# One core, a retention layer and two mixture layers in one launch: lam is loaded from ScalarE's queue, and VectorE instead of GpSimd decays the first chunk's keys of five heads

## The chip, the cores and the metric

The kernel runs on one core of one Trainium2 chip. The time is the device time of one launch in microseconds (us); the number that counts is the median of several runs. A core has TensorE (PE; its weight loads are shown apart as PEld), VectorE (DVE), ScalarE (ACT), GpSimd (POOL) and SyncE (SP), and 16 DMA engines that all its queues share. SyncE here does nothing but start DMAs; ScalarE can start DMAs too, on a queue of its own.

## The reference

Three layers follow one another. Only the first matters for the change: a retention layer with one decay factor `lam` per head, worked through block by block with a running state `kv_state`.

```
for b in range(nb):
    intra = einsum('bhic,bhjc->bhij', qb, kb) * Dmask      # Dmask: powers of lam below the diagonal
    intra = einsum('bhij,bhjd->bhid', intra, vb)
    inter = einsum('bhid,bhde->bhie', qb * lam_pow, kv_state)
    out[:, :, sl] = intra + inter
    kb_dec = kb * rev_pow                                  # keys decayed by powers of lam
    kv_state = lam_block * kv_state + einsum('bhsd,bhse->bhde', kb_dec, vb)
```

There are 2 sequences of 768 positions and 8 heads of width 64. Two layers of matrix products come after it: a normalised two-matrix layer with residual (512 to 2048 to 512), and a routed attention over 4 experts.

## The kernel before

The retention layer is done in 12 chunks of 128 positions (6 for each sequence, taken in turn, so that chunk 0 and chunk 1 are both of the first sequence). Each chunk has two loads of 512 KB: `qk` (queries and keys, transposed; `load_qk`, L149) and `kvn` (keys and values; `load_kv`, L159). All loads are started by SyncE, on its one queue, in program order, several ahead of their use; a buffer that is still read holds back the load into it and all that stand behind it on the queue.

Everything that involves the decay is made from `lq`, a copy of `lam` (32 bytes) in each of the 128 partitions, loaded by one small DMA (L317). From `lq` VectorE makes `dec` with 8 scans, one for each head (L341), and GpSimd makes `qpow` with two copies and 7 doublings (L343, L346).

The first 20 to 50 us of the program are written out by hand: the string FRONT is a list of tokens that are emitted in that order, and the program order is the order on each engine (manual schedule). The tokens that matter here, each with the chunk's number n:

- `q:n`, `k:n`: start the load of `qk` or `kvn` of chunk n. The very first `qk` load stands right behind that of `lam`.
- `R:n`, `S:n`: scores `sc` on TensorE (L366, L370). `A:n`: `a` = scores times `dec` on VectorE (L401).
- `Ka:n`, `Kg:n`: the decayed keys `kd`; three heads by ScalarE (L389), the other five by GpSimd in one instruction (L395). There are two `kd` buffers.
- `T:n`: the chunk's share of the state, `ps`, on TensorE from `kd` and `kvn` (L415). `D:n` makes the state `st` from it on VectorE (L442, L444), `O:n` decays it to `old` on GpSimd (L450).
- `U:n`, `I:n`: the output `po` on TensorE, from the old state (L425) and from `a` (L434). `C:n` copies it to `xT` on ScalarE (L458, L460).

TensorE starts the program with ten matmuls on zeros (`warma`, L135), which feed nothing. Chunk 3's buffers are part of a tile named `early`. `g_sb` is a small constant that ScalarE loads (L693) for the layer behind. The order on TensorE is: `warma`, scores of chunk 0, `ps` of 0, `po` of 0, `ps` of 1, `ps` of 2, scores of 1 and 2, `po` of 1 and 2, and so on. Behind the retention layer TensorE goes on with the matmuls of the second layer (`h`, `y`) and of the third.

Of the kernel before, what the change touches and what calls it, by code (L numbers as in the profile page):

```python
# [14 lines left out]
ALU = mybir.AluOpType  # L15
AX = mybir.AxisListType

P = 128
B, H, S, D = 2, 8, 768, 64
# [55 lines left out]


FRONT = """
    k:0 Ka:0 Kg:0 k:1 k:2 Kg:1 q:1 R:0 Ka:1 A:0 Ka:2 T:0 D:0 I:0 C:0 Kg:2 O:0 T:1 T:2 D:1 S:1 q:2 w q:3 q:4 A:1 k:3
    k:4 S:2 A:2 Q:1 Q:2 O:1 D:2 Q:4 U:1 I:1 z:0 Q:3 O:2 l:0 t:0 U:2 I:2 C:1 w R:3 R:4 A:3 C:2 A:4 G Kg:3 ma:0 W mc:0
    mm:0 mi:0:0 h:0 r:0 k:5 q:5 U:3 I:3 e:0 Ka:3 T:3 Kg:4 k:6 D:3 O:3 Ka:4 T:4 S:5 A:5 U:4 C:3 q:6 Kg:6 q:7 sq:0:0  # L80
    Q:5 I:4 w z:1 mi:0:1 R:6 D:4 U:5 I:5 xs:0:0 k:7 xs:0:1 C:4 k:8 k:9 Ka:6 q:8 q:9 T:6 A:6 Q:7 C:5 I:6 D:6 k:10 p:0
# [17 lines left out]
def model(ctx, tc, qkT, kv, lam, g_ln, w12, wat, out):  # L99
    nc = tc.nc  # L100
# [31 lines left out]
    def warm(n, name):  # L132
        ps = ps_mid(f"warm{name}")
        for _ in range(n):
            nc.tensor.matmul(ps, zeros[:, :P], zeros, start=True, stop=True)  # L135
# [3 lines left out]
    R = {}  # L139
# [3 lines left out]
    def load_qk(n):  # L143
        b, c = order[n]
        if n % 4 == 3:
            qk = early[:, 0].rearrange("p (a h i) -> p a h i", a=2, h=HP)
        else:
            qk = r2.tile([P, 2, HP, P], F32, tag="qk", name=f"qk{b}{c}", bufs=3)
        nc.sync.dma_start(qk, qkT[b, c])  # L149
        R.setdefault((b, c), {})["qk"] = qk  # L150

    def load_kv(n):
        b, c = order[n]
        if n % 4 == 3:
            kvn = early[:, 1].rearrange("p (a h d) -> p a h d", a=2, h=H)
        else:
            kvn = r2.tile([P, 2, H, D], F32, tag="kvn", name=f"kvn{b}{c}", bufs=3)
        if c < NC - 1:
            nc.sync.dma_start(kvn, kv[b, c])  # L159
        else:  # L160
            nc.sync.dma_start(kvn[:, 1], kv[b, c, :, 1])
        R.setdefault((b, c), {})["kvn"] = kvn
# [56 lines left out]
    n, free_at = PLAN_FROM, 0  # L219
# [19 lines left out]
    def load_next(k=1):  # L239
        for _ in range(k):  # L240
            if to_load:
                to_load.pop(0)()
# [57 lines left out]
    def prep():  # L300
# [9 lines left out]
    lq = rc.tile([P, H], F32, tag="lq", name="lq")  # L310
    dec = rc.tile([P, H, P], F32, tag="dec", name="dec")
# [2 lines left out]
    by_hand = ExitStack()  # L314
    by_hand.enter_context(tc.manual_schedule(engines={
        mybir.EngineType.SP, mybir.EngineType.DVE, mybir.EngineType.Activation, mybir.EngineType.Pool}))
    nc.sync.dma_start(lq, lam.rearrange("h o -> o h").to_broadcast([P, H]))  # L317
    load_qk(0)
    g_sb = const.tile([P, KT], F32, tag="g", name="g_sb")
    table = const.tile([P, 1], F32, tag="table", name="table")  # L320
# [40 lines left out]
    def ret_scores(n, whole=False):  # L361
        r = R[order[n]]
        sc = r["sc"] = ps_big(f"sc{n}")
        for hp, h2 in HEADS:
            if whole:
                nc.tensor.matmul(sc[:, h2, cols(hp)], r["qk"][half(h2), 1, hp, :], r["qk"][half(h2), 0, hp, :],  # L366
                                 start=True, stop=True, skip_group_check=True)
                continue
            for kh in range(2):
                nc.tensor.matmul(sc[half(kh), h2, cols(hp)], r["qk"][half(h2), 1, hp, half(kh)],  # L370
                                 r["qk"][half(h2), 0, hp, :], start=True, stop=True, skip_group_check=True)

    def ret_qd(n):
        b, c = order[n]
        if c > 0:
            r = R[b, c]
            r["qd"] = r2.tile([P, HP, P], F32, tag="qd", name=f"qd{n}")
            nc.gpsimd.tensor_tensor(r["qd"], r["qk"][:, 0], qpow, ALU.mult)

    def ret_kd(n):  # L380
        r = R[order[n]]
        r["kd"] = r2.tile([P, H, D], F32, tag="kd", name=f"kd{n}")

    def ret_kd_some(n):
        r = R[order[n]]
        if "kd" not in r:
            ret_kd(n)
        for h in range(3):
            nc.scalar.mul(r["kd"][:, h, :], r["kvn"][:, 0, h, :], dec[:, h, P - 1:P])  # L389

    def ret_kd_rest(n):
        r = R[order[n]]
        if "kd" not in r:
            ret_kd(n)
        nc.gpsimd.tensor_tensor(r["kd"][:, 3:, :], r["kvn"][:, 0, 3:, :],  # L395
                                dec[:, 3:, P - 1:P].to_broadcast([P, H - 3, D]), ALU.mult)

    def ret_decay(n):
        r = R[order[n]]
        a = r["a"] = r2.tile([P, 2, HP, P], F32, tag="a", name=f"a{n}")  # L400
        nc.vector.tensor_mul(a, r["sc"].rearrange("p h (k i) -> p h k i", k=HP),  # L401
                             dec.rearrange("p (h k) i -> p h k i", h=2))
# [5 lines left out]
    def ret_state(n):  # L408

        b, c = order[n]  # L410
        r = R[b, c]
        if c < NC - 1:
            ps = r["ps"] = ps_mid(f"ps{n}")
            for hp, h2 in HEADS:
                nc.tensor.matmul(ps[half(h2), cols(hp, D)], r["kd"][:, h2 * HP + hp, :],  # L415
                                 r["kvn"][:, 1, h2 * HP + hp, :], start=True, stop=True, skip_group_check=True)

    def ret_outer(n):
        b, c = order[n]
        r = R[b, c]  # L420
        r["po"] = ps_big(f"po{n}")
        if True:
            st = ST.pop(n - 1)
            for hp, h2 in HEADS:
                nc.tensor.matmul(out_at(r["po"], hp, h2), st[half(h2), hp, :], r["qd"][half(h2), hp, :],  # L425
                                 start=(hp < 2), stop=False, skip_group_check=True)

    def ret_inner(n):
        b, c = order[n]
        r = R[b, c]  # L430
        if c == 0:
            r["po"] = ps_big(f"po{n}")
        for hp, h2 in HEADS:
            nc.tensor.matmul(out_at(r["po"], hp, h2), r["kvn"][:, 1, h2 * HP + hp, :], r["a"][:, h2, hp, :],  # L434
                             start=(c == 0), stop=True, skip_group_check=True)

    def ret_sum(n):
        b, c = order[n]
        st = ST[n] = r2.tile([P, HP, D], F32, tag="st", name=f"st{n}")
        pv = R[b, c]["ps"][:, :HP * D].rearrange("p (h e) -> p h e", h=HP)  # L440
        if c == 0:
            nc.vector.tensor_copy(st, pv)  # L442
        else:
            nc.vector.tensor_tensor(st, pv, ST["old"], ALU.add)  # L444

    def ret_old(n):
        st = ST[n]
        if True:
            ST["old"] = r2.tile([P, HP, D], F32, tag="old", name=f"old{n}", bufs=1)
            nc.gpsimd.tensor_tensor(ST["old"], st, qpow[:, :, P - 1:P].to_broadcast([P, HP, D]), ALU.mult)  # L450
# [26 lines left out]
    def ln_copy(blk, name):  # L477
        s4 = LN[name, blk] = lnp.tile([P, TB], F32, tag="s4", name=f"{name}s{blk}")
        nc.scalar.copy(s4, LP.pop((name, blk))[:, :TB])
# [193 lines left out]
    def do(op, *a):  # L673
        if op == "q":
            load_qk(*a)
        elif op == "k":
            load_kv(*a)
        elif op == "w":
            load_next()
        elif op == "S":  # L680
            ret_scores(*a)
        elif op == "R":
            ret_scores(*a, whole=True)
        elif op == "A":
            ret_decay(*a)
        elif op == "Ka":
            ret_kd_some(*a)
        elif op == "Kg":
            ret_kd_rest(*a)
        elif op == "Q":  # L690
            ret_qd(*a)
        elif op == "G":
            nc.scalar.dma_start(g_sb, g_ln)  # L693
        elif op == "W":
            warm(WARM[1], "b")
        elif op == "U":
            ret_outer(*a)
        elif op == "T":
            ret_state(*a)
        elif op == "I":  # L700
            ret_inner(*a)
        elif op == "D":
            ret_sum(*a)
        elif op == "O":
            ret_old(*a)
        elif op == "C":
            ret_copy(*a)
        elif op == "ma":
            ln_sums(*a, "mu")
        elif op == "mc":  # L710
            ln_copy(*a, "mu")
        elif op == "mm":
            ln_mean(*a)
        elif op == "mi":
            ln_minus(*a)
        elif op == "xs":
            ln_high(*a)
        elif op == "lo":
            ln_low(*a)
        elif op == "sq":  # L720
            ln_square(*a)
        elif op == "va":
            ln_sums(*a, "va")
        elif op == "vc":
            ln_copy(*a, "va")
        elif op == "vd":
            ln_out(*a)
        elif op == "P":
            begin(a)
        elif op == "LA":  # L730
            LEAVE[a][0]()
        elif op == "LD":
            LEAVE[a][1]()
        elif op == "X":
            rp.close()
            rest_of_room()
        elif op == "park":
            park(*a)
        else:
            PARTS[a[0]]["zlthrep".index(op)]()  # L740
# [329 lines left out]
```

## Time and profile before

| | |
|---|---|
| median of 3 runs | 448.39 us (448.27 to 448.59) |
| profiled execution | 448.26 us; its span, from the first to the last instruction, 446.5 us |
| TensorE (PE) busy | 440.2 us, 99% of the span |
| VectorE, ScalarE, GpSimd busy | 314.2 us, 201.7 us, 38.0 us |
| DMA, 0 to 60 us | 16.94 MB, 282 GB/s |

The profile is of one execution. Busy time is the time in which an engine's instructions were running; a bracket at the end of a row tells how long the engine had been idle before it and what ended the idle time. Times are counted from the start of the span.

### The profile page before, as it was taken

What the parts mean: (1) busy time and instruction counts of PE and PEld (TensorE: products, weight loads), DVE (VectorE), ACT (ScalarE), POOL (GpSimd) and SP (SyncE); (2) the same over time, 40 slices, a digit from 0 to 9 for tenths busy, and PEclk for the clock granted to TensorE, in tenths of its full rate; (3) what the DMA queues carried; (4) which work ended last, traced back from release to release, by engine and by line L of the source; (5) the groups of instructions that cost most, each with busy time, mean ns of one, the idle gap of its engine ahead of it and who ended that gap; (6) DMA issues with size and microseconds to landing.
All of it is one profiled execution on the core that took longest, in us unless ns stands there. A gap on an engine that the chain in (4) does not pass through costs nothing.

```text
span 446.5 us, 9085 instructions
## 1 busy us (share of the span) xinstructions
PE 440.2 (99%) x3714; PEld 414.0 (93%) x3715; DVE 314.2 (70%) x622; ACT 201.7 (45%) x464; POOL 38.0 (9%) x64
## 2 busy tenths in 40 slices
PE   8999999999999999999999999999999999999997
PEld 5678889999999999999999999999999998999885
DVE  4689899859768778626799936556657485756753
ACT  4488765445433213202324612212146657747872
POOL 7655200000000000000000000000000100001000
PEclk9999999999999999999999999999999999999999
DMA  7985643514321231201132531211000000001012
GB/s 294 391 332 214 189 144 112 182 41 155 130 94 54 88 95 51 91 0 46 50 102 87 186 99 52 73 56 35 1 1 0 1 2 2 25 25 48 25 72 97
DMA packets 15226, 41.81 MB, mean 94 GB/s; under 512 B 2240, under 2 KB 5072, under 8 KB 15184
## 3 DMA queue, kind: packets, MB, share of 16 engines
q1 hardware_dynamic: 14896, 41.10, 27.1%
q8 instruction: 29, 0.48, 0.4%
q10 hardware_dynamic: 288, 0.13, 0.1%
q14 instruction: 13, 0.11, 0.1%
HBM read 34.90 MB, written 6.32 MB: 92 GB/s over the span
## 4 chain that ended last, share of the span: by engine, by line
PE 94%; DMA 2%; ACT 1%; POOL 1%; DVE 1%; issue 0%; DVEq 0%; ACTq 0%
PE h L556 30%; PE y L592 28%; PE pj L818 8%; PE av L961 4%; PE pv L833 4%; PE o L988 4%; PE s L896 4%; PE t L949 3%; PE po L434 2%; PE yf L614 2%; PE sc L366 1%; DMA kvn<-in_kv 1%; PE po L425 1%; PE mean L483 1%; DMA lq<-in_lam 1%; PE ps L415 1%
## 5 line engine op out<-in xcount | busy, mean ns | idle before, releaser
L556 PE MATMUL h<-xn,w 128*128 128x384 f32 x768 | 138.5, 335 | 0.0
L556 PEld LDWEIGHTS h<-xn,w 128*128 128x128 f32 x768 | 133.5, 188 | 1.4 <-issue 0.6
L592 PE MATMUL y<-hs,w 128*128 128x384 f32 x552 | 99.7, 334 | 0.0
L592 PEld LDWEIGHTS y<-hs,w 128*128 128x128 f32 x552 | 96.1, 188 | 0.0
L575 ACT ACTIVATE hs<-h 128x384 fp32r<-128x384 f32 x50 | 24.5, 491 | 113.6 <-PE h L556 104.1
L578 DVE SCALAR_TENSOR_TENSOR hs<-h,hs 128x384 fp32r<-128x384 f32 x50 | 27.7, 554 | 33.2 <-ACT hs L575 33.2
L600 DVE TENSOR_TENSOR xT<-xT,y 128x768 f32<-128x768 f32 x24 | 22.8, 951 | 27.3 <-PE y L592 27.3
L920 POOL TENSOR_TENSOR wide<-c,gw 128x256 f32<-128x256 f32 x12 | 7.3, 612 | 382.2 <-DVE c L917 359.0
L818 PE MATMUL pj<-x,wa 128*128 128x384 f32 x192 | 35.1, 338 | 0.0
L818 PEld LDWEIGHTS pj<-x,wa 128*128 128x128 f32 x192 | 33.3, 188 | 0.5 <-ACT gw L859 0.2
L278 ACT CAST w<-top 128x512 fp32r<-128x512 f32 x32 | 19.8, 618 | 30.4 <-DVE top L270 30.4
L951 ACT COPY aT<-t 128x384 f32<-128x384 f32 (+5 forms) x68 | 28.1, 467 | 8.2 <-PE t L949 8.1
L261 ACT ACTIVATE mag<-raw 128x512 f32<-128x512 f32 x31 | 20.5, 669 | 7.9 <-DVE w L289 4.1
L286 DVE TENSOR_TENSOR top<-top,w 128x512 f32<-128x512 f32 x32 | 21.9, 684 | 0.8 <-ACT w L278 0.8
L289 DVE TENSOR_TENSOR w<-top,mag 128x512 fp32r<-128x512 f32 x32 | 22.0, 686 | 0.3
L283 DVE SCALAR_TENSOR_TENSOR mag<-raw,mag 128x512 f32<-128x512 uint32 x31 | 21.4, 689 | 0.7
L270 DVE SCALAR_TENSOR_TENSOR top<-raw,mag 128x512 int32<-128x512 int32 x31 | 21.4, 689 | 0.6
L961 PE MATMUL av<-aT,v 128*64 128x128 f32 x336 | 20.6, 276 | 0.0
L903 ACT ACTIVATE att<-s,negm 128x384 f32<-128x384 f32 (+3 forms) x32 | 16.7, 531 | 7.8 <-DVE negm L901 7.4
L896 PE MATMUL s<-k,qs 64*128 64x384 f32 (+4 forms) x192 | 20.1, 334 | 0.0
L961 PEld LDWEIGHTS av<-aT,v 128*64 128x64 f32 x336 | 18.1, 137 | 1.5 <-issue 1.0
L949 PEld LDWEIGHTS t<-ident,att 64*128 64x128 f32 x336 | 14.8, 138 | 4.7 <-issue 2.8
(140 smaller groups left out, 622.5 us busy)
## 6 DMA issues: line engine op xcount, KB each, us to landing
raw<-in_w SPq DMA_DIRECT2D x31, 512.0 KB, 3.7
qk<-in_qkT SPq DMA_DIRECT2D x9, 512.0 KB, 7.6
kvn<-in_kv SPq DMA_DIRECT2D x8, 512.0 KB, 6.6
xd<-xT SPq DMA_DIRECT2D x4, 768.0 KB, 8.0
xr<-xd SPq DMA_DIRECT2D x8, 384.0 KB, 3.1
out<-os SPq DMA_DIRECT2D x11, 256.0 KB, 2.0
early<-in_qkT SPq DMA_DIRECT2D x3, 512.0 KB, 7.9
rawa<-in_wat SPq DMA_DIRECT2D x3, 512.0 KB, 3.3
```

Source lines behind the costliest of these rows:

```text
L286: nc.vector.tensor_tensor(t["top"], t["top"], t["w"][:, 0].bitcast(F32), ALU.subtract)
L289: nc.vector.tensor_tensor(t["w"][:, 1], t["top"], t["mag"], ALU.add)
L556: nc.tensor.matmul(ph[:, :TB], w[:, wi, k, :], xn[:, xi, k, :], start=(i == 0), stop=(i == 11))
L575: LAST.append([nc.scalar.activation(h[:, 0], ph[:, :TB], AF.Relu)])
L578: LAST[-1].append(nc.vector.scalar_tensor_tensor(h[:, 1], ph[:, :TB], 0.0, h[:, 0].bitcast(F32), ALU.max, ALU.subtract))
L592: nc.tensor.matmul(y[:, j, :TB], w[:, wi, e * P:(e + 1) * P], h[:, xi], start=(f == 0 and i == 0), stop=(f == GF - 1 and i == 2))
L600: nc.vector.tensor_tensor(xv, xv, y[:, :, :TB], ALU.add)
L818: nc.tensor.matmul(ps[:, :TB], w[:, wi, k, :], x2[:, xi, k, :], start=(i == 0), stop=(i == 11))
L896: nc.tensor.matmul(banks[h][c], q[r, qi], k[r, ki, pr, c * m:(c + 1) * m], start=(i == 0), stop=(i == 2))
L949: nc.tensor.transpose(pt[r][:, j], x[half(r)], ident[half(r), half(r)])
L951: nc.scalar.copy(aT[:, :, r], pt[r])
L961: nc.tensor.matmul(row["pav"][half(e2), pr * P:(pr + 1) * P], v[:, j, e * HD:(e + 1) * HD], row["aT"][pr][:, (e2 * (t + 1) + j) * P:(e2 * ...
```

## The change

The load of `lam` is started by ScalarE, on ScalarE's own DMA queue, and no longer by SyncE. `Kg:0`, the decay of the first chunk's keys of heads 3 to 7, becomes `Kv:0`: the same instruction on VectorE. The other chunks keep GpSimd.

```
 FRONT = """
-    k:0 Ka:0 Kg:0 k:1 k:2 Kg:1 q:1 R:0 Ka:1 A:0 Ka:2 T:0 D:0 I:0 C:0 Kg:2 O:0 T:1 T:2 D:1 S:1 q:2 w q:3 q:4 A:1 k:3
+    k:0 Ka:0 Kv:0 k:1 k:2 Kg:1 q:1 R:0 Ka:1 A:0 Ka:2 T:0 D:0 I:0 C:0 Kg:2 O:0 T:1 T:2 D:1 S:1 q:2 w q:3 q:4 A:1 k:3
...
-    nc.sync.dma_start(lq, lam.rearrange("h o -> o h").to_broadcast([P, H]))
+    nc.scalar.dma_start(lq, lam.rearrange("h o -> o h").to_broadcast([P, H]))
     load_qk(0)
...
-    def ret_kd_rest(n):
+    def ret_kd_rest(n, engine):
         r = R[order[n]]
         if "kd" not in r:
             ret_kd(n)
-        nc.gpsimd.tensor_tensor(r["kd"][:, 3:, :], r["kvn"][:, 0, 3:, :],
-                                dec[:, 3:, P - 1:P].to_broadcast([P, H - 3, D]), ALU.mult)
+        engine.tensor_tensor(r["kd"][:, 3:, :], r["kvn"][:, 0, 3:, :],
+                             dec[:, 3:, P - 1:P].to_broadcast([P, H - 3, D]), ALU.mult)
...
         elif op == "Kg":
-            ret_kd_rest(*a)
+            ret_kd_rest(*a, nc.gpsimd)
+        elif op == "Kv":
+            ret_kd_rest(*a, nc.vector)
```

On ScalarE, at the very start of the program (`table` is a one-column copy that brings in the activation table; the branch is the program's first jump, whose line number alone has changed):

```order
-L1066 UNCONDITIONAL_BRANCH
+L1068 UNCONDITIONAL_BRANCH
+L317 DMA lq<-in_lam 128x8
 L321 ACT_TABLE_LOAD
 L321 CAST table<-zeros 128x1
```

The start of the DMA comes ahead of everything that ScalarE does; it waits for nothing. On SyncE, at the same place, the first row goes and the loads of chunk 0 are the first that its queue gets:

```order
-L1066 UNCONDITIONAL_BRANCH
-L317 DMA lq<-in_lam 128x8
+L1068 UNCONDITIONAL_BRANCH
 L149 DMA qk_113<-in_qkT 128x1024
 L159 DMA kvn_162<-in_kv 128x1024
```

On VectorE, from the program's start to the first chunk's state (kd of chunk 0 is named `kd_164`, its `kvn` `kvn_162`):

```order
 L130 MEMSET zeros 128x256
 L341 SCALAR_TENSOR_TENSOR dec<-lq,hit 128x128 x8
+L395 TENSOR_TENSOR kd_164<-kvn_162,dec 128x320
 L401 TENSOR_TENSOR a_189<-sc_177,dec 128x1024
 L442 COPY st_204<-ps_195 128x256
```

The decay of five heads' keys now stands between the eight scans and `a` of chunk 0; on GpSimd the same row is gone from its place behind the last doubling of `qpow`.

## Rows read from the trace of the kernel before

**Rows 1.** Windows: busy us (instructions) of PE, PEld, DVE, ACT, POOL; clock; DMA share; GB/s.

```profile
40.00:60.00 20.00, 20.00 (x249) 17.62 (x248) 18.15 (x30) 15.32 (x34) 5.04 (x5) 1.00 0.50 166
60.00:300.00 240.00, 240.00 (x1392) 237.44 (x1391) 174.88 (x311) 80.66 (x145) 0.00 (x0) 1.00 0.28 88
```

**Rows 2.** The chain that ended last, its first 50 us: start, us, what.

```profile
0.74 2.72 DMA lq<-in_lam
...
9.31 0.74 POOL kd L395
...
10.09 0.68 PE ps L415 x14
...
11.87 1.24 DVE a L401
...
29.42 5.35 DMA kvn<-in_kv
```

**Rows 3.** Timeline, 0 to 14 us: start, us, engine, instruction, count [idle before].

```profile
0.74 0.39 SPq L317 DMA_DIRECT2D lq<-in_lam  x1
...
1.19 0.41 SPq L149 DMA_DIRECT2D qk<-in_qkT  x1
...
3.56 2.85 DVE L341 TENSOR_TENSOR_SCAN dec<-lq,hit 128x128 f32<-128x128 f32 x8 [2.43 <-DMA lq<-in_lam]
...
4.05 2.76 POOL L346 TENSOR_TENSOR qpow<-qpow 128x4 f32<-128x4 f32 x7
...
4.86 0.44 SPq L149 DMA_DIRECT2D early<-in_qkT  x1
...
5.56 1.02 PEld L366 LDWEIGHTS sc<-qk 64*128 64x128 f32 x16 [0.84 <-DMA qk<-in_qkT]
...
6.68 0.82 ACT L389 ACTIVATE kd<-kvn,dec 128x64 f32<-128x64 f32 x3 [4.46 <-DMA kvn<-in_kv]
6.78 0.72 POOL L395 TENSOR_TENSOR kd<-kvn,dec 128x320 f32<-128x320 f32 x1
...
6.83 1.22 DVE L401 TENSOR_TENSOR a<-sc,dec 128x1024 f32<-128x1024 f32 x1 [0.43 <-PE sc L366]
...
10.09 0.54 PEld L415 LDWEIGHTS ps<-kvn,kd 128*64 128x64 f32 x14 [0.24 <-POOL kd L395]
```

**Rows 4.** DMA packets of 2.2 to 3.3 us, then of 3.4 to 4.4 us.

```profile
DMA packets 103, 0.07 MB, mean 62 GB/s; under 512 B 87, under 2 KB 87, under 8 KB 103
...
DMA packets 93, 0.38 MB, mean 381 GB/s; under 512 B 0, under 2 KB 0, under 8 KB 93
```

**Rows 5.** ScalarE's other early DMA; then chunk 3's `qk`: KB, us to landing.

```profile
16.62 0.39 ACTq L693 DMA_DIRECT2D g_sb<-in_g_ln  x1
...
early<-in_qkT SPq DMA_DIRECT2D x1, 512.0 KB, 9.8
```

**Rows 6.** DMA by queue (q1 SyncE's, q10 ScalarE's), 19.9 to 21.9 us; then 21.9 to 23.1.

```profile
q1 hardware_dynamic: 211, 0.77, 96.9%
q10 hardware_dynamic: 138, 0.00, 4.1%
...
q10 hardware_dynamic: 6, 0.00, 0.5%
```

**Rows 7.** VectorE by line and form, 0 to 60 us: count, busy us, mean ns, idle before.

```profile
L444 DVE TENSOR_TENSOR st<-ps,old 128x256 f32<-128x256 f32 x8 | 3.4, 419 | 2.6 <-POOL old L450 2.0 <-PE ps L415 0.6
...
L286 DVE TENSOR_TENSOR top<-top,w 128x512 f32<-128x512 f32 x3 | 2.1, 684 | 0.0
```

**Rows 8.** Lines 500 and 450 alone: shortest/median/longest ns, first and last start.

```profile
L500 DVE SCALAR_TENSOR_TENSOR xn<-dq,g_sb,xn x8: 608/612/1083, 30.8 to 51.0; 128x384 fp32r<-128x384 f32 x8
...
L450 POOL TENSOR_TENSOR old<-st,qpow x8: 621/638/941, 10.0 to 43.9; 128x256 f32<-128x256 f32 x8
```

**Rows 9.** Timelines of VectorE and GpSimd at 30 us.

```profile
30.83 0.98 DVE L500 SCALAR_TENSOR_TENSOR xn<-dq,g_sb,xn 128x384 fp32r<-128x384 f32 x1
...
30.46 0.94 POOL L450 TENSOR_TENSOR old<-st,qpow 128x256 f32<-128x256 f32 x1
```

## The prediction

> **What bounds the kernel now.** The windows come first [rows 1]: from 40 us on TensorE is never idle, 20.00 of 20.00 us and then 240.00 of 240.00. What comes earlier or later at 40 us therefore comes earlier or later at the end, and the change sits in the first 10 us. Next the chain that ended last [rows 2]. It begins with the load of `lam`, goes through GpSimd, the first chunks' states on TensorE, VectorE's `a` of chunk 1 and, from 29.42 us, the load of chunk 9's keys, which starts when TensorE has freed the buffer. So the start is a chain of TensorE with short stalls, and it begins with `lam`. The timeline shows the first links [rows 3]: `lam` is issued at 0.74 us and has landed at 0.74 + 2.72 = 3.46 [rows 2]; VectorE's eight scans run from 3.56 to 6.41; GpSimd's doublings run from 4.05 to 6.81; the first `qk` lets TensorE's scores start at 5.56; the first keys are there at 6.68; `a` of chunk 0 starts at 6.83.
>
> **What the change takes away.** SyncE's queue loses one issue: the first `qk` is issued at 0.74 instead of 1.19, and all the loads behind it can be 0.45 us earlier [rows 3]. Little of that can be used. Earlier scores are of no use, since `a`, which takes them, also needs the scans; these depend on `lam` alone and end at 6.41 at the earliest. The place that can use it is chunk 2: its five decayed heads run on GpSimd from 9.31 [rows 2], and TensorE stands idle 0.24 us for them [rows 3]. With chunk 2's keys 0.45 us earlier, and one instruction of 0.72 us less on GpSimd [rows 3], that stall goes: **-0.24**. ScalarE issues `lam` ahead of its activation table; it is idle for 4.46 us before its first decayed keys [rows 3], so the 0.39 us of issuing costs nothing; without that idle time it would cost these 0.39.
>
> **What it adds on VectorE.** The decay of 320 columns goes in front of `a`. VectorE does 256 columns in 419 ns and 512 in 684 [rows 7], so 320 take 419 + 265/4 = 485 ns. Before, VectorE was idle for 0.43 us ahead of `a` [rows 3], so most of it is hidden, if nothing else is in the way. Something is. The decay reads two operands from SBUF while GpSimd's last doubling still runs, until 6.81. Where such a pair met [rows 9], both were longer: VectorE's line 500 took 0.98 us (median 612 ns), GpSimd's line 450 took 0.94 (median 638) [rows 8]. That is 0.3 to 0.37 us each. The doubling leaves 6.81 - 6.41 = 0.40 us to be met, so the wait lies between 0 and 0.40; I take 0.25, because a part of the doubling's time is its start. `a` then starts at 6.41 + 0.05 + 0.49 + 0.25 = 7.20 instead of 6.83, **+0.37**, and `po` of chunk 0 and all behind it on TensorE with it.
>
> On this wait the Trainium skill (SBUF — State Buffer, section "Who interferes with whom") is stricter: a VectorE instruction with two SBUF inputs and a GpSimd one that reads SBUF exclude each other for the whole instruction. By that the wait would be the full 0.40 and the sum 0.15 higher.
>
> **What it does to the arrival of `lam`.** This is the largest term, and the trace holds no case of two loads that start together on two queues. Before, `lam`'s 128 small rows stood alone at the head of the only queue; the loads of chunk 0 came behind them. Now they start at the same time as 512 KB of `qk` on the other queue, on the same 16 engines. Two things are to be seen. First, the first rows of `qk` are slow: from 2.2 to 3.3 us there are 103 - 87 = 16 large packets, one for each engine, at 62 GB/s; from 3.4 us on the rate is 381 [rows 4]. Full rate thus comes 2.2 us after the issue at 1.19, and would come at 2.95 after an issue at 0.74. Second, the one other load that ScalarE issues early is as small as `lam`: `g_sb`, issued at 16.62 in the middle of SyncE's traffic [rows 5]. Its packets pass from 19.9 us on between the large ones, 138 small to 211 large in 2.0 us, and the last six only after 21.9 [rows 6]. It took over 5.3 us instead of `lam`'s 2.72. A small transfer on the second queue is not let past the large ones.
>
> The price: an engine has 128/16 = 8 rows of `lam`. If each waits for one large packet, and a large packet takes 16 x 2.0/211 = 0.152 us [rows 6], the eight need 1.2 us from 2.95 on, which is 4.15; with 0.25 from the last row to the landing it is 4.4 instead of 3.46: **+0.95**. The bounds: below 0, if `lam`'s rows get through while the first rows of `qk` are still on their way; an earlier landing than 3.46 is excluded, since ScalarE can't issue before 0.74 and there is nothing that would make 128 rows faster than alone. Above, as `g_sb`: up to 23.1 - 16.62 = 6.5 us, which is 3.8 more. I take 0.95 because the queues are still empty at the start, while `g_sb` met a full one. The scans and the doublings both hang on `lam`, so both move by it, and `a` with them.
>
> **Other waits.** By the order of the changed program ScalarE's `g_sb` DMA now waits for chunk 3's `qk` load to land; that is 4.86 + 9.8 = 14.7 us [rows 3, 5], well before 16.62, so nothing behind it on ScalarE (its copy of the first means, the next decayed keys) is held. Chunk 4's key load now waits for VectorE instead of GpSimd to have read chunk 0's keys; it waits for `po` of chunk 0 anyway, which comes after both.
>
> **The sum.** +0.95 (`lam`) + 0.37 (VectorE) - 0.24 (stall of chunk 2) = +1.08 us at `ps` of chunk 2. From there the chain is TensorE, `a` of chunk 1 at 11.87, TensorE, and the load at 29.42 that TensorE itself releases [rows 2]; I see no wait on it for something that does not move along, so it is carried to 40 us and to the end. The profiled execution took 448.26: 449.34. It lies 0.13 below the median of the runs, 448.39, so I predict 449.5. A change within 0.2% (0.90 us, 447.49 to 449.29) is about what a measurement of this kernel can't tell from none.
>
> **The rivals.**
> - *`lam` is not delayed* (on the other side: not slower). Its eight rows on each engine pass before the first row of `qk` has its data. Then only -0.24 and VectorE's 0.12 to 0.52 remain: -0.12 to +0.28, so 448.3 to 448.7, no change that can be told. For it speaks that the engines move next to nothing until 3.3 us [rows 4]; against it, that those first 16 packets occupy them all the same. It decides as long as `lam` lands less than 0.75 us late. The Trainium skill (DMA: Bandwidth & Descriptors, section "Queues, rings and completion order") speaks for this rival: an engine takes turns between its queues by whole packets of some 9 to 17 descriptors, so that all of `lam`'s rows on an engine could go in one turn. The trace of `g_sb` rather shows single rows between large ones.
> - *`lam` comes behind a backlog*, as `g_sb` did: SyncE keeps issuing 512 KB every 0.45 us, and `lam` waits behind two or more of them. 2 to 3.8 us late gives 450.5 to 452.3.
> - *The earlier loads pay off.* Every wait for a load goes down by 0.45, `lam` comes in time and VectorE's decay meets nothing: 447.9. To be faster by more than 0.2% it would need twice what the queue gives; TensorE's waits in this stretch are single ones of 0.2 to 0.3 us like the 0.24 of chunk 2 [rows 3].
>
> **How the numbers follow.** The forecast case (`lam` 0.7 to 1.4 us late) gives 0.7 - 0.12 to 1.4 + 0.28 = +0.6 to +1.7, so 449.0 to 450.1; chance 0.50, of which 0.08 lie within 0.2%. `lam` not delayed: 0.30, all within. The backlog: 0.10, slower. The pay-off: 0.10, of which 0.04 beyond 0.2%. Slower 0.42 + 0.10 = 0.52; same 0.08 + 0.30 + 0.06 = 0.44; faster 0.04. The range from 448.2 to 450.4 takes in the first two cases and leaves out the rest of the other two; the forecast's own range is 449.0 to 450.1.
>
> **What would show it.** `lam` landed, and the first scan started, near 4.4 us instead of 3.46: this step alone decides. VectorE's decay of 0.5 us, or 0.7 where it meets the last doubling; `a` of chunk 0 near 8.2; no stall of TensorE for chunk 2's GpSimd keys; the chunk 9 load issued near 30.5; the first `h` matmuls some 1.1 us later than before. The prediction is wrong if `lam` lands before 4.2 us, or if a wait behind 10 us is for something that has not moved and takes up the delay.

## The result, and the profile after

The changed kernel takes 452.58 us (median of 5 runs, 451.72 to 453.02) against 448.39: a ratio of 1.0092 with a 95% interval of 1.0081 to 1.0103. It is slower by 0.9%, which is the sign that was forecast, but 452.58 lies 3.1 us above the predicted 449.5 and outside the range of 448.2 to 450.4. The profiled run took 451.72 us, its span 449.9 us, 3.4 more than before.

The chain that ended last, in the changed kernel (start, us, what), answers to [rows 2]:

```profile
0.74 5.45 DMA lq<-in_lam
...
9.17 0.72 DVE kd L395
9.90 1.14 DVE a L401
...
11.08 1.97 PE po L434 x16
...
16.75 0.67 PE po L425 x16
...
32.87 5.22 DMA kvn<-in_kv
```

It begins with `lam` as before, but `lam` lands at 0.74 + 5.45 = 6.19 us, where it landed at 3.46: +2.73. The first matmuls of `U` for chunk 1 (L425) go from 13.24 to 16.75, +3.51, and the load of chunk 9's keys from 29.42 to 32.87, +3.45. The sixteen matmuls of chunk 0's `po` (L434) take 1.97 us; before they took 1.09. The first `h` matmuls of the second layer go from 39.62 to 43.06, +3.44. These are the rows of the timeline of before for `po`, `U` and `h`, and last that of the changed kernel for `h`:

```profile
8.11 1.09 PE L434 MATMUL po<-a,kvn 128*64 128x128 f32 x16
...
13.24 0.67 PE L425 MATMUL po<-qd,st 64*64 64x128 f32 x16 [0.30 <-DVE a L401]
...
39.62 1.66 PE L556 MATMUL h<-xn,w 128*128 128x384 f32 x8
...
43.06 1.14 PE L556 MATMUL h<-xn,w 128*128 128x384 f32 x5
```

The first 12 us of the timeline (start, us, engine, instruction, count, idle before) answer to [rows 3]:

```profile
0.74 0.41 ACTq L317 DMA_DIRECT2D lq<-in_lam  x1
0.74 0.39 SPq L149 DMA_DIRECT2D qk<-in_qkT  x1
...
6.06 1.48 PE L366 MATMUL sc<-qk 64*128 64x128 f32 x16 [0.43 <-DMA qk<-in_qkT]
...
6.29 2.85 DVE L341 TENSOR_TENSOR_SCAN dec<-lq,hit 128x128 f32<-128x128 f32 x8 [5.16 <-DMA lq<-in_lam]
6.79 2.76 POOL L346 TENSOR_TENSOR qpow<-qpow 128x4 f32<-128x4 f32 x7
...
9.17 0.72 DVE L395 TENSOR_TENSOR kd<-kvn,dec 128x320 f32<-128x320 f32 x1
9.51 0.98 POOL L395 TENSOR_TENSOR kd<-kvn,dec 128x320 f32<-128x320 f32 x1
9.82 1.21 DVE L401 TENSOR_TENSOR a<-sc,dec 128x1024 f32<-128x1024 f32 x1
...
9.95 0.96 PE L415 MATMUL ps<-kvn,kd 128*64 128x64 f32 x14 [1.66 <-DVE kd L395]
```

Three things are to be seen. The first `qk` is issued 0.45 us earlier, and yet the scores that need it start 0.50 us later, 6.06 instead of 5.56: the large load came late too, not only the small one. `a` of chunk 0 starts at 9.82 instead of 6.83, +2.99, so VectorE's extra decay adds only 2.99 - 2.73 = 0.26. And TensorE is idle for 1.66 us ahead of `ps`. The DMA packets of 2.2 to 3.3 us, and then of 3.4 to 4.4 us, answer to [rows 4] (q1 is SyncE's queue, q10 ScalarE's; packets, MB, share of the 16 engines):

```profile
DMA packets 80, 0.18 MB, mean 161 GB/s; under 512 B 37, under 2 KB 37, under 8 KB 80
...
q1 hardware_dynamic: 43, 0.18, 58.1%
q10 hardware_dynamic: 37, 0.00, 1.7%
...
DMA packets 70, 0.13 MB, mean 128 GB/s; under 512 B 39, under 2 KB 39, under 8 KB 70
...
q1 hardware_dynamic: 35, 0.13, 50.5%
q10 hardware_dynamic: 35, 0.00, 1.6%
```

Where the kernel before moved 381 GB/s, this one moves 128, and the two queues pass packets in equal numbers: in 1.0 us 35 of `lam`'s rows on q10, and 35 on q1, of which 31 are large (39 packets are under 512 B, the 35 rows and 4 others). The windows (busy us and instructions of PE, PEld, DVE, ACT, POOL; granted clock; DMA share; GB/s) answer to [rows 1]:

```profile
9.00:10.00 1.00, 0.05 (x2) 0.05 (x2) 0.96 (x3) 0.61 (x3) 1.00 (x2) 1.00 1.05 430
10.00:11.00 1.00, 0.91 (x14) 0.72 (x14) 1.00 (x2) 0.00 (x1) 0.48 (x1) 0.59 1.02 418
11.00:12.00 1.00, 0.92 (x10) 0.92 (x11) 0.37 (x2) 0.82 (x3) 0.95 (x2) 0.50 1.04 422
12.00:13.00 1.00, 1.00 (x14) 1.00 (x14) 0.00 (x0) 0.00 (x0) 1.00 (x2) 0.50 1.02 406
13.00:14.00 1.00, 1.00 (x31) 1.00 (x28) 0.06 (x1) 0.87 (x3) 1.00 (x2) 0.71 1.05 418
...
40.00:60.00 20.00, 20.00 (x273) 16.89 (x268) 18.21 (x28) 15.90 (x37) 7.66 (x8) 1.00 0.55 186
60.00:300.00 240.00, 240.00 (x1392) 237.44 (x1391) 177.79 (x316) 83.10 (x150) 0.00 (x0) 1.00 0.28 90
```

From 40 us to 300 TensorE is never idle here either. But behind the idle stretch TensorE's granted clock is 0.50, its lower level of 1.2 GHz, for about 3 us; before, it was 1.00 in every microsecond from 8 to 17 us, as in this one:

```profile
10.00:11.00 1.00, 0.91 (x26) 0.84 (x30) 0.35 (x1) 0.98 (x4) 1.00 (x3) 1.00 1.04 418
```

That the prediction did not have at all.

### The profile page after: what moved, and what is told of

Its sections match the earlier page's. It is cut to its first block, busy times and chain, and to the rows that moved or that the text cites. A ratio compares the mean times of both kernels' runs of the same rounds, so it can differ in the third digit from the quotient of the medians.

```text
span 449.9 us, 9088 instructions
## 1 busy us (share of the span) xinstructions
PE 441.5 (98%) x3715; PEld 415.1 (92%) x3715; DVE 316.4 (70%) x623; ACT 202.0 (45%) x464; POOL 38.3 (9%) x63
## 4 chain that ended last, share of the span: by engine, by line
PE 93%; DMA 2%; DVE 2%; ACT 2%; issue 0%; POOL 0%; DVEq 0%; ACTq 0%
PE h L556 30%; PE y L592 28%; PE pj L820 8%; PE av L963 4%; PE pv L835 4%; PE o L990 4%; PE s L898 4%; PE t L951 3%; PE po L434 2%; PE yf L614 2%; DMA lq<-in_lam 1%; PE sc L366 1%; DMA kvn<-in_kv 1%; PE po L425 1%; PE mean L483 1%; DVE dec L341 1%
## 5 line engine op out<-in xcount | busy, mean ns | idle before, releaser
L270 DVE SCALAR_TENSOR_TENSOR top<-raw,mag 128x512 int32<-128x512 int32 x31 | 22.3, 720 | 0.6
L286 DVE TENSOR_TENSOR top<-top,w 128x512 f32<-128x512 f32 x32 | 21.9, 684 | 0.8 <-ACT w L278 0.8
L289 DVE TENSOR_TENSOR w<-top,mag 128x512 fp32r<-128x512 f32 x32 | 21.9, 686 | 0.3
```

Of the source, the lines that this page charges most:

```text
L270: nc.vector.scalar_tensor_tensor(t["top"].bitcast(I32), RAW[ft, i][:, :, 1], -0x40000000, t["mag"].bitcast(I32), ALU.bitwise_and, ALU.bitw ...
L286: nc.vector.tensor_tensor(t["top"], t["top"], t["w"][:, 0].bitcast(F32), ALU.subtract)
```

## The experiments

Twelve kernels were run. Each is compared with the kernel before on the same chip (448.3 to 448.5 us there).

**The two halves of the change.** First the load alone; the decay of chunk 0 goes back to GpSimd:

```
-    k:0 Ka:0 Kv:0 k:1 ...
+    k:0 Ka:0 Kg:0 k:1 ...
```

> Only lam's load is moved to ScalarE's queue; GpSimd keeps the first chunk's five heads. Theory A (small rows of lam and large rows of qk take turns on every DMA engine when both loads start together): lam lands near 6.2 us as with the whole change, not at 3.46, and the time is 451.0 to 453 us, most of the whole change's loss. Rival B (the loss comes from VectorE's decay in front of a, and lam's late landing is hidden): below 449.3 us.

452.62 us (451.83 to 454.21, 5 runs), ratio 1.01 [1.0085, 1.0115]. In the profiled run, one of 453.53 us, `lam` lands at 6.27 us, TensorE is idle 1.92 us ahead of `ps`, and the clock is 0.50 from about 8.2 to 15 us. The load alone costs as much as the whole change. Then the other half; `lam` goes back to SyncE:

```
-    nc.scalar.dma_start(lq, lam.rearrange("h o -> o h").to_broadcast([P, H]))
+    nc.sync.dma_start(lq, lam.rearrange("h o -> o h").to_broadcast([P, H]))
```

> Only the first chunk's five heads go to VectorE; lam stays on SyncE's queue. Theory A: lam lands at 3.46 us as before, VectorE's decay takes 0.5 to 0.75 us behind the scans, a of chunk 0 starts near 7.2 us instead of 6.83 and chunk 2's stall on GpSimd stays as its keys come no earlier: 448.3 to 449.0 us. Rival B: 451 us or more.

448.27 us (448.22 to 448.56, 11 runs), ratio 1.0001 [0.9993, 1.0010]: no change. Its timeline shows why:

```profile
6.72 0.56 DVE L395 TENSOR_TENSOR kd<-kvn,dec 128x320 f32<-128x320 f32 x1 [0.20 <-DMA kvn<-in_kv]
...
7.21 1.21 DVE L401 TENSOR_TENSOR a<-sc,dec 128x1024 f32<-128x1024 f32 x1
...
8.47 1.09 PE L434 MATMUL po<-a,kvn 128*64 128x128 f32 x16 [0.42 <-DVE a L401]
...
9.35 0.73 POOL L395 TENSOR_TENSOR kd<-kvn,dec 128x320 f32<-128x320 f32 x1 [0.57 <-DMA kvn<-in_kv]
```

`a` is 0.38 us later than the 6.83 of [rows 3], and `po` of chunk 0 0.36 later. Chunk 2's decay on GpSimd is no earlier than before (9.35 against 9.31) and through at 10.08; but TensorE now comes to it later, and its stall of 0.24 us is gone, which was not expected. The first `U` matmuls start at 13.28 against 13.24: TensorE's delay is taken up where it had waited.

**Is ScalarE's queue slow by itself?** SyncE is made to start a 4-byte transfer first that waits for `zeros`. So it starts `qk` only at 1.51 us, while `lam` is started by ScalarE at 0.73 and has 0.78 us ahead:

```
+    late = dram.tile([1, 2], BF16, tag="late", name="late")
+    nc.sync.dma_start(late, zeros[:1, :2])
     load_qk(0)
```

> The whole change, but SyncE first starts a DMA of 4 bytes that waits for the zeros, so that the first qk load is issued near 1.5 us and lam, alone on ScalarE's queue, at 0.74. Theory A: lam's rows are through, or nearly so, before those of qk come, it lands between 3.4 and 4.3 us, and the time is 448.3 to 450 us. Rival C (ScalarE's queue is slow for lam whatever SyncE does): lam lands near 6.2 us and the time is 451.5 us or more.

448.67 us (448.30 to 449.70, 11 runs), ratio 1.0009 [1.0001, 1.0018]. In the profiled run, the one of 449.70 us, the first scan starts at 3.37 us, 0.19 earlier than before. The packets of 2.2 to 3.3 us, then those of 3.4 to 4.4:

```profile
q1 hardware_dynamic: 20, 0.08, 61.9%
q10 hardware_dynamic: 87, 0.00, 3.6%
...
DMA packets 93, 0.38 MB, mean 381 GB/s; under 512 B 0, under 2 KB 0, under 8 KB 93
```

87 packets of ScalarE's queue pass in the time in which the changed kernel passed 37. The queue is not slow; the meeting of `lam` with the large loads is.

**Is it the common start?** `lam` is started behind the activation table, so that it meets loads that already run:

```
-    nc.scalar.dma_start(lq, lam...)
     load_qk(0)
...
     nc.scalar.copy(table, zeros[:, :1])
+    nc.scalar.dma_start(lq, lam...)
```

> The whole change, but ScalarE starts lam's load behind its activation table, near 2.2 us, when SyncE's queue holds three or four loads. If only a common start is slow, the rate stays near 400 GB/s from 3.4 us on, and lam lands between 5 and 9 us, as g_sb did behind a full queue (5.3 to 6.5 us after its issue). If small rows cost 0.3 us each wherever they meet large ones, the rate falls below 200 GB/s for the 3 to 4 us in which lam's rows pass.

One run of 453.82 us. `lam` is issued at 1.17 and lands 5.84 us later. The same two stretches:

```profile
DMA packets 97, 0.40 MB, mean 361 GB/s; under 512 B 0, under 2 KB 0, under 8 KB 97
...
DMA packets 78, 0.06 MB, mean 63 GB/s; under 512 B 63, under 2 KB 63, under 8 KB 78
```

The large loads run at 361 GB/s until `lam`'s rows arrive, and fall to 63 in that microsecond. It isn't the start. Nor do small and large rows pass in equal numbers here: of the 78 packets of the second stretch 63 are small.

**Is it a fixed delay, or each row?** The same load twice on ScalarE's queue, the first into a tile that nothing reads, so 16 rows for each engine instead of 8:

```
+    lq2 = rc.tile([P, H], F32, tag="lq2", name="lq2")
+    nc.scalar.dma_start(lq2, lam.rearrange("h o -> o h").to_broadcast([P, H]))
```

> The whole change, with a second copy of lam into a tile that nothing reads, loaded on ScalarE's queue ahead of the first: 16 instead of 8 small rows for each engine. Theory A (small rows and large rows take turns one for one, and a pair costs about 0.46 us while both queues have rows at the start): lam lands near 9 to 9.8 us and the DMA rate stays below 200 GB/s until then. Rival D (a fixed delay of some 2.7 us, whatever the number of rows): lam lands at 6.2 to 6.8 us.

One run of 454.23 us. `lam` lands at 8.27, 2.1 us after the 6.19 of the changed kernel, which is between the two forecasts: eight rows more cost 0.26 us each. In 3.4 to 4.4 us 36 small rows of q10 pass to 34 large packets. So every row costs, though the later ones less than the 16 x 1.0/35 = 0.46 us that a row took in this stretch of the changed kernel.

**Is it the second queue?** `lam` goes back to SyncE, and ScalarE starts a load of 512 KB, `kvn` of chunk 0, behind the table (`load_kv` gets the queue as an argument):

```
-    k:0 Ka:0 Kv:0 k:1 ...
+    Ka:0 Kv:0 k:1 ...
...
-    nc.scalar.dma_start(lq, lam...)
+    nc.sync.dma_start(lq, lam...)
...
+    load_kv(0, nc.scalar)
```

> lam is back on SyncE's queue, ahead of all; the 512 KB of chunk 0's keys and values come from ScalarE's queue instead, issued behind its activation table near 2.2 us, so that large rows of two queues meet. VectorE keeps the five heads. If any two queues that meet at the start halve the rate, it is below 250 GB/s from 3.4 to 4.4 us and after; if the small rows are the cause, the rate is 370 to 430 GB/s from 3.4 us on, and lam lands at 3.5 us.

One run of 449.60 us. From 3.4 to 4.4 us 48 large packets of q1 and 39 of q10 pass, at 356 GB/s. That is a little under the 370 expected for small rows as the cause, and far above the 250 for any two queues. Two queues of large rows share the engines at near full rate; `qk` comes later for it (scores at 6.74). It takes small rows, or these small rows.

**Small rows, or `lam`'s?** The load of `g_sb`, 128 rows of 16 bytes, is started behind the table instead of at 16.62 us; `lam` is back on SyncE and `Kv:0` stays:

```
     nc.scalar.copy(table, zeros[:, :1])
+    nc.scalar.dma_start(g_sb, g_ln)
...
         elif op == "G":
-            nc.scalar.dma_start(g_sb, g_ln)
+            pass
```

> lam is back on SyncE's queue, Kv:0 stays, and the load of g_sb (128 rows of 16 bytes, each from an address of its own) is issued by ScalarE right behind its activation table instead of at 16.6 us. It should be issued near 1.17 us, beside the first large load (1.19). Theory 'any 128 small rows that run beside the first large loads slow them': the rate of 3.4 to 4.4 us falls far below the 381 GB/s of before, to 60 to 200, small and large packets come in about equal numbers, scores start at 6 us or later and the time is 449 to 452. Rival 'it is something of lam's own (all its 128 rows read the same 32 bytes)': the rate stays at 350 to 400 GB/s as it did at 19.9 us in the kernel before, scores start near 5.6 and the time is within 0.2% of before.

One run of 448.61 us; the kernel before beside it took 448.54. `g_sb` lands 3.2 us after its issue at 1.17, scores start at 5.65, and from 3.4 to 4.4 us the rate is 283 GB/s with 46 packets of q10 to 69 of q1. The time is the rival's and the rate between the two. But `lam`'s own rows came ahead of `qk` on q1 while `g_sb`'s ran, so this did not settle it, and two more kernels differ from each other in nothing but the address. In both SyncE starts `qk` and `kvn` of chunk 0 ahead of `lam` (so `lam` comes late, and the time tells nothing here), and ScalarE starts 128 rows of 16 bytes at 0.74 into a tile `gx` that nothing reads. In the first every row has its own address, in the second all are read from the first row:

```
+    nc.scalar.dma_start(gx, g_ln)
```

```
+    nc.scalar.dma_start(gx, g_ln[0:1].to_broadcast([P, KT]))
```

> A measurement of the second queue alone, not a candidate. SyncE starts qk of chunk 0 first, then kvn of chunk 0, and only then lam, so that lam is late by design (7 us or more) and the time is above before by some us. ScalarE's first instruction is a load of 128 rows of 16 bytes, each from an address of its own (a second copy of g_sb, which nothing reads), issued at 0.74 beside qk as lam was in the changed kernel. Theory 'any 128 small rows beside the first large loads': as with lam, 100 to 180 GB/s from 3.4 to 4.4 us, about as many small as large packets, landing some 5 us after the issue. Rival 'that all rows read one address': 300 GB/s or more from 3.4 to 4.4 us, landing about 3 us after the issue.

> The same kernel as the one beside it but for the address: ScalarE's 128 rows of 16 bytes are all read from the first row of g_ln, as lam's 128 rows all read the same 32 bytes. Theory 'that all rows read one address': 100 to 180 GB/s from 3.4 to 4.4 us, landing some 5 us after the issue, where the kernel beside it shows 300 GB/s or more and 3 us. Rival 'any 128 small rows': no difference between the two.

455.56 and 456.80 us, one run each. The packets of 2.2 to 3.3 us and of 3.4 to 4.4 us with 128 addresses:

```profile
DMA packets 156, 0.33 MB, mean 299 GB/s; under 512 B 76, under 2 KB 76, under 8 KB 156
...
DMA packets 174, 0.41 MB, mean 410 GB/s; under 512 B 74, under 2 KB 74, under 8 KB 174
...
q1 hardware_dynamic: 116, 0.41, 100.4%
q10 hardware_dynamic: 58, 0.00, 3.3%
```

and with one address:

```profile
DMA packets 89, 0.21 MB, mean 194 GB/s; under 512 B 37, under 2 KB 37, under 8 KB 89
...
DMA packets 72, 0.14 MB, mean 144 GB/s; under 512 B 37, under 2 KB 37, under 8 KB 72
...
q1 hardware_dynamic: 36, 0.14, 57.2%
q10 hardware_dynamic: 36, 0.00, 1.6%
```

This is the answer. With 128 addresses the same number of small rows leaves the large loads at 410 GB/s; with one address they run at 144, with 36 packets to 36 as in the changed kernel (each kernel is one profiled run, but the two rates are far apart). A large packet itself gets longer, 16 x 0.572/35 = 0.26 us against 16 x 1.004/100 = 0.16 (35 of the 72 packets and 100 of the 174 are large), and with one address packets fill only 57.2% and 1.6% of the engines' time. The first of the two kernels shows the same on SyncE's own queue: there `lam` comes behind `kvn`, and from 4.4 to 6 us, while 84 small packets pass on q1, the rate is 99 GB/s (in the kernel before, 26 small packets and 420 GB/s in this stretch):

```profile
DMA packets 122, 0.16 MB, mean 99 GB/s; under 512 B 84, under 2 KB 84, under 8 KB 122
```

So it takes no second queue either.

**Without the copies.** This kernel keeps the whole change, but loads one row of `lam`; TensorE spreads it over the partitions by a row of ones, between the fifth and the sixth zero matmul:

```
+    nc.scalar.dma_start(lq1, lam.rearrange("h o -> o h"))
...
+    nc.tensor.matmul(pl[:, :H], ones, lq1, start=True, stop=True)
...
-    nc.scalar.dma_start(lq, lam.rearrange("h o -> o h").to_broadcast([P, H]))
+    nc.vector.tensor_copy(lq, pl[:, :H])
```

> lam stays on ScalarE's queue and Kv:0 on VectorE, but only one row of 32 bytes is loaded; TensorE spreads it over the 128 partitions with one matmul by a row of ones between the fifth and the sixth zero matmul, and VectorE copies it from PSUM to lq. Theory 'it is the 128 reads of one address, not the queue': the large loads run at 300 to 400 GB/s from 2.4 us on, qk has landed before 5.5 us, the first scan starts at 3.2 to 3.7 us, no half clock, and the time is 447.7 to 448.5, that is within 0.2% of before or just better. Rival 'a small load on the second queue comes late whatever it is': lam lands after 5 us, the scans start after 5.5 and the time is 450 or more.

449.08 us (448.67 to 449.37, 11 runs), ratio 1.0015 [1.0006, 1.0024]: 3.5 us less than the changed kernel. Its timeline, and its packets of 2.2 to 3.3 us:

```profile
3.43 0.59 PE L143 MATMUL lamps<-lq,ones 1*128 1x8 f32 x2
...
4.34 2.85 DVE L348 TENSOR_TENSOR_SCAN dec<-lq,hit 128x128 f32<-128x128 f32 x8
...
7.22 0.72 DVE L402 TENSOR_TENSOR kd<-kvn,dec 128x320 f32<-128x320 f32 x1
```

```profile
DMA packets 96, 0.39 MB, mean 357 GB/s; under 512 B 0, under 2 KB 0, under 8 KB 96
```

`lam` has landed by 3.43 us on the same queue, beside `qk`, which now runs at 357 GB/s in this stretch. The clock is 1.00 in every window. The first scan is not where it was expected: the matmul and the copy put it at 4.34, 0.78 later than before, and the time is 0.71 above before and outside what was expected. So the cause is confirmed, and nothing is gained: no kernel here beats the one before, and the decay on VectorE alone equals it.

**What the lower clock costs.** First six more of the zero matmuls at the start:

```
-WARM = (10, 3)
+WARM = (16, 3)
```

> The whole change, with 16 instead of 10 matmuls on zeros ahead of the scores, which fill TensorE's idle time before the first chunk's state is ready. lam lands near 6.2 us as before. If the fall of the granted clock to half from 10.2 to 13.6 us follows from that idle time, the clock stays at 1.00 and the time is some 0.8 us or more below the whole change's (450.3 to 451.7 us). If the clock falls for another reason, the time is the same as the whole change's, 452 to 453 us.

451.79 us (450.21 to 452.18, 6 runs), ratio 1.0068 [1.0056, 1.0081]. In the profiled run, one of 452.08 us, the sixteen end at 6.77 us and TensorE is still idle for 1.62 us ahead of `ps` at 9.95; the clock falls to 0.50 later, from 12 to 15 us. The stretch that mattered was not filled. Over a whole run the mean granted clock was 0.996 in three of the six (452.08 to 452.18 us) and 0.999 or 1.000 in the other three (450.21 to 451.50): 1.1 us between their medians. Then eleven zero matmuls between the scores and `ps`, where the idle time lies, to see whether the clock stays up:

```
-    ... q:1 R:0 Ka:1 A:0 ...
+    ... q:1 R:0 V Ka:1 A:0 ...
...
+        elif op == "V":
+            warm(11, "c")
```

> The whole change, with 11 matmuls on zeros on TensorE between the scores and the state of chunk 0, where it stood idle for 1.66 us with lam late. lam still lands near 6.2 us. [...]

450.77 us (450.70 to 452.59, 5 runs), ratio 1.0060 [1.0046, 1.0074]. Two windows of the profiled run, and its first `U` matmuls:

```profile
9.00:10.00 1.00, 1.00 (x6) 0.39 (x4) 0.96 (x3) 0.75 (x3) 0.92 (x3) 1.00 1.01 414
10.00:11.00 1.00, 0.79 (x16) 0.54 (x14) 1.00 (x2) 0.13 (x1) 0.72 (x2) 1.00 1.02 418
...
15.74 0.67 PE L425 MATMUL po<-qd,st 64*64 64x128 f32 x16 [0.56 <-DVE a L401]
```

`lam` lands no earlier (6.34), but the clock stays at 1.00 (its mean is 0.999 or 1.000 in all five runs, against 0.992 to 0.996 in those of the changed kernel), `po` of chunk 0 takes 1.09 us again, and the median is 1.81 us below the changed kernel's. So the idle time is what brings the clock down. How much that costs is less sure. The profiled run is the one of 452.59 us: it is 2.50 us behind the kernel before at the first `U`, and loses more only later (TensorE is idle for 1.3 us between 44 and 50 us, waiting for GpSimd's `qd` and for a copy of ScalarE). And one run of the kernel with the load alone took 452.62 us at a mean clock of 1.000.

## Why the prediction was wrong

**The step that failed** is the price of `lam`'s arrival, +0.95; it measured +2.73. It had two parts. That about one large packet passes for each of `lam`'s rows was right for this stretch: 35 rows to 31 large packets. The start and the time of a pair were wrong. The prediction read [rows 4] as "the first rows of `qk` are slow" and let full rate begin 2.2 us after the issue. But the 62 GB/s of that row were made by `lam`, not by `qk`: without the 128 copies `qk` runs at 357 GB/s in the same microsecond, and at 235 from 1.7 to 2.8 us, which is as long after its issue as that row is. So `lam` is a load that slows the large loads beside it, and what the change did was to set it beside `qk`, which was thereby drawn out too. The kernel before pays for it too: with one row the keys of chunk 0 are there by 5.46 us instead of 6.68, though their load is issued only 0.45 earlier. And 0.152 us for a packet came from `g_sb`'s stretch [rows 6], whose 128 rows have 128 addresses (18 of the 211 packets were small as well, so a large one took 0.166); beside `lam` a pair took 0.46 us. Eight pairs from 2.2 us on are 2.2 + 8 x 0.46 = 5.9, near the 6.19 of the landing. This 0.46 is read from the changed kernel itself and is no constant: the second copy's rows cost 0.26 each. `g_sb` was the nearest row by size and by queue, and it was the wrong one: what mattered was what it reads.

**What was missed** is the clock, a term that the sum did not have. TensorE's wait of 1.66 us was not itself the last cost: behind it the granted clock was 0.50, and `po` of chunk 0 took 1.97 us instead of 1.09, +0.88 in the profiled run. The way from `po` of chunk 0 to the first `U` took 16.75 - 11.08 = 5.67 us; with the idle time filled and the clock at 1.00 it took 15.74 - 11.24 = 4.50, and before 13.24 - 8.11 = 5.13. So the profiled runs add up: 11.08 - 8.11 = 2.97 at `po`, 1.17 for the clock, and 5.13 - 4.50 = 0.63 given back on the way make +3.51 at the first `U`. By the medians it is 1.81, with the spread that the experiment shows.

**What held, and what only came out right.** VectorE's decay was priced at 0.485 us and 0.25 more where it meets the doubling: 0.49 us alone (in the staggered kernel), 0.72 where it met the last 0.38 us of it. The Trainium skill (SBUF — State Buffer, section "Who interferes with whom") would have had it wait for the whole 0.38; it lost 0.23. GpSimd's next decay, beside it and beside `a`, took 0.98 instead of 0.73 us, so the price is paid on both sides, as in [rows 9]. Of +0.37 for `a`, +0.26 was measured in the changed kernel. The +0.38 with `lam` in its place is partly luck: there the scans ended 0.11 later, VectorE waited 0.20 us for the load of the keys, which the prediction had not priced, and the decay took 0.56, as it met only the last 0.22 of the doubling.

The stall of chunk 2, -0.24, went as well, but no run shows that it went for the reason given, earlier keys. In the kernel with the decay alone GpSimd's keys came no earlier; TensorE came later. In the staggered kernel, where GpSimd has one instruction less too, the stall is still there:

```profile
10.33 0.54 PEld L417 LDWEIGHTS ps<-kvn,kd 128*64 128x64 f32 x14 [0.24 <-POOL kd L397]
```

So it was slack that a late TensorE uses up, a part of the 0.63 given back.

That a delay at the start is carried to the end held in the changed kernel: `h` +3.44, the span +3.4; and the kernel with one row started its scans 0.78 later and took 0.71 longer. It isn't carried one for one in every run: the profiled run of the staggered kernel is 0.24 behind at the first `U` (13.48) and 1.4 at the span, that of the kernel with the stretch filled 2.50 and 4.3.

**The rivals.** "`lam` is not delayed" fell. By the Trainium skill (DMA: Bandwidth & Descriptors, section "Queues, rings and completion order") all eight rows on an engine could go in one turn. In the changed kernel they did not: `lam`'s load ends with sixteen packets of 4 bytes, and the first of them comes at 4.56 us, when 86 of the 128 rows have passed, so that no engine was through with its share by then. Where `lam` was started behind the table, the first of the sixteen comes after 31 rows; there the eight of an engine may have gone together, and `lam` was no less late for it. "`lam` behind a backlog" had the size: `lam`'s 2.73 lies within its 2 to 3.8, and its 450.5 to 452.3 ends just below the measured time. That is luck, since the reason is another. `lam`'s rows pass from 2.2 us on, so they did not wait behind two loads; and started behind loads that already ran, `lam` took 5.84 us, hardly more than the 5.45 beside the first of them, and its own rows brought the rate down from 361 to 63 GB/s. "The earlier loads pay off" did not happen, since `qk` came later.

**What stays open** is where the reads of one address are held up, at the memory or in the DMA engines. The runs show that the address decides, and nothing further. Copies of `lam` at 128 addresses weren't tried, since the input holds it once.

## What to carry to other kernels

A load that copies one row to all partitions is small in bytes and not in cost: look at the rate of the large loads in the microsecond in which it runs, and set it where nothing large runs beside it, or load one row and spread it on chip. When a small transfer is priced by another one in the trace, compare what they read, not only size and queue. And where a delay opens an idle stretch on TensorE, look at the granted clock behind it: here it made 1.2 of the 3.5 us by which the profiled run was late at the first `U`.

## What the runs showed of the hardware that was not expected

- 128 rows of 16 bytes from one address, beside 512 KB loads: 144 GB/s from 3.4 to 4.4 us; 128 such rows from 128 addresses: 410 GB/s. It happens with two queues and with one (99 GB/s, with `lam`'s rows of 32 bytes).
- A DMA that stands behind the activation table's load on ScalarE is issued at 1.17 us, while that load runs from 0.73 to 2.01 (in three of the kernels): it does not wait for it.
- TensorE's granted clock fell to its lower level near 10.2 us, behind idle stretches of 0.43 and 1.66 us that two matmuls part, and was back at 1.00 in the window from 14 us. With six more zero matmuls ahead of the same 1.62 us it fell later, in the window from 12 us; with the stretch filled it did not fall. With the load alone moved it fell near 8.2 us, behind idle stretches of 0.79 and 0.83 us on either side of the scores, and ahead of the long one of 1.92.
